# Attention and two MLP layers on one core: the scores of two units issued together from the eighth pair on, and the odd transpose of the tail unit made 128 wide

## The chip, the cores and the metric

One NeuronCore of a Trainium2 chip runs the program. The metric is the device time of one execution in microseconds; the kernel before took 975.68 us (median of three runs, 975.42 to 976.11).

## What is computed

Attention over 4 batches and 8 heads, 576 positions, 64 columns per head, then two MLP layers on 2304 tokens, all in fp32:

```
scores = q k^T / sqrt(D) + min(bias, 0),  bias = -(cum[i] - cum[j]),  cum = cumsum(max(s, 0))
attn   = softmax(scores, causal)
x      = attn v                       # 2304 x 512
x      = leaky_relu(x w_in, 0.01) w_out      # 512 -> 2048 -> 512
out    = softplus(x w2_in) w2_out            # 512 -> 2048 -> 512
```

## The kernel before

The work of the attention stage goes by **pairs** of heads, 16 of them; the two heads of a pair lie in the lower and the upper 64 partitions. A pair has four **units** of queries, in this order: block 3 (queries 384 to 511, four blocks of keys, 512 columns), the tail (the last 64 queries of both heads, 576 keys, laid out as two halves of 288 columns), block 2 (384 columns), and blocks 1 and 0 (256 and 128 columns). Each unit goes through: `scores` on TensorE (lines 311 and 297; Q.K, then a second matmul with BQ and BK that adds the decay; scores use 64 rows of the array, both heads side by side), `maxima` on VectorE (line 332, it also writes the scaled scores into the SBUF tile `sc`), `exps` on ScalarE (line 344), `divisors` on VectorE (lines 350 and 351), `norm` on GpSimd (line 355), `transpose` on TensorE (lines 372, 367 and 363, whole array) into a PSUM tile `pt_t`, and `evacuate`, a copy into PA, PB or PZ: on ScalarE (line 384) for the even half of a unit and for both halves of block 3, on VectorE (line 386) for the rest. `pv` (line 403, 64 columns of the array) multiplies the copies with V. Most of these come in two halves, j = 0 and 1, for the two heads; for the tail unit the even half has four transposes (line 367) and the odd half one (line 363).

The order of all engines is written out by hand in one loop over steps n. In step n the scores of unit n+1 are issued, unit n goes through maxima and exps, unit n-1 is normalised, unit n-2 is transposed, and the last copy of unit n-3 is made. `tick()` runs what earlier steps put off. In the middle of each step `fill.step(n)` issues one half of an MLP matmul group of the first layer (a **chunk**: six matmuls of 512 columns, lines 145 and 614) for a batch that is done; it also loads and splits weights in some steps. A group's two halves fill one PSUM bank (tag `m`, one buffer), which ScalarE empties one tick after the second half. Output groups are not issued before all four hidden tiles are ready; until then a step has no chunk. PV comes at the end of every second step.

Three pools matter: `sc` has three buffers, the transposes' PSUM tag `t` has two, and each of the score tags `s0` and `s1` has two.

After the last pair come the rest of the first layer and the second layer, from about 246 us to the end: MLP matmuls without a break.

Of the kernel before, what the change touches and what calls it, by code (L numbers as in the profile page):

```python
# [18 lines left out]
P = 128  # L19
# [6 lines left out]
def view(t, offset, *dims):  # L26

    return bass.AP(t.tensor, t.offset + offset, [list(t.ap[0])] + [list(d) for d in dims])
# [3 lines left out]
def attn_moe_moe(ctx, tc, q, k, v, s, w1i, w1o, w2i, w2o, out):  # L32
    nc = tc.nc

    B, H, S = s.shape
# [7 lines left out]
    NP = B * NPAIR  # L43
    NB = S // P
    TL = S - NB * P
# [26 lines left out]
    def tick():  # L72
        clock[0] += 1
        for fn, args in todo.pop(clock[0], ()):
            fn(*args)
# [5 lines left out]
    def move(dst, src, queue=nc.sync):  # L81
        queue.dma_start(dst.bitcast(F32), src.bitcast(F32))
# [72 lines left out]
    def attention(att, ps, fills):  # L155
        ident = att.tile([P, P], F32, tag="ident", name="ident")
# [5 lines left out]
        two = lambda nm, shape, dt=F32: [att.tile(shape, dt, tag=f"{nm}{i}", name=f"{nm}{i}") for i in range(2)]  # L162
# [7 lines left out]
        PZ = att.tile([P, 2, TL], F32, tag="PZ", name="PZ")  # L170
# [5 lines left out]
        one = view(V[1], 0, [1, S])  # L176
        s0, s1 = (view(att.tile([P, 2, 512], F32, tag="sc", name="sc", bufs=3), 0, [1, S]) for _ in range(2))
# [52 lines left out]
            nc.sync.dma_start(c_d, c1)  # L230

        def zeros():
            nc.gpsimd.memset(PZ[TL:], 0.0)

        def heads(p):
            b, hp = divmod(p, NPAIR)
# [2 lines left out]
        def load(p, nm, queue=nc.sync, c=slice(None)):  # L239
            if p < NP:  # L240
                t, x = {"q": (Q, q), "k": (K, k), "v": (V, v)}[nm]
                queue.dma_start(t[p % 2][:, c], x[p, :, c])

        def rows(p):

            if p < NP:
                b, hs = heads(p)
                for j in range(2):
                    h, r = b * H + hs.start + j, j * D
                    move(BK[p % 2][r:r + 2], bb_d[h, :, :SB])  # L250
                    move(BQ[p % 2][r + 32:r + 34], bb_d[h, :, :SB])

        def decays(p):

            if p < NP:
                o = c_d.offset + p * 2 * S
                for j in range(2):
                    nc.sync.dma_start(M[p % 2][j * D:(j + 1) * D], bass.AP(c_d.tensor, o + j * S, [[0, D], [1, S]]))
# [8 lines left out]
        def bias(p):  # L267
            if 0 < p < NP:
                m = M[p % 2]
                nc.vector.tensor_scalar(m, m, CQ[:, p:p + 1], None, op0=ALU.subtract)  # L270
                later(1, nc.gpsimd.tensor_tensor, m[:, SB:], m[:, SB:], maskl[:, SH - TL:], ALU.add)


        class Unit:
# [82 lines left out]
            def transpose(self, j):  # L357
                sc = self.sc
                pt = ps.tile([P, 512], F32, tag="t", name="pt_t", bufs=2)
                if self.last:  # L360
                    sc = view(sc, 0, [1, S])
                    if j:
                        nc.tensor.transpose(pt[:TL, :P], sc[:, NB * P:S], ident)
                        self.outs = PZ[:TL], pt[:TL, :P].rearrange("p (j x) -> p j x", x=TL)
                        return
                    for c in range(NB):
                        nc.tensor.transpose(pt[:, c * P:(c + 1) * P], sc[:, c * P:(c + 1) * P], ident)  # L367
                    self.outs = PA[:, :, :, P:], pt.rearrange("p (c j x) -> p j c x", j=2, x=TL)
                    return
                n = self.W // P  # L370
                for c in range(n):
                    nc.tensor.transpose(pt[:, c * P:(c + 1) * P], sc[:, j, c * P:(c + 1) * P], ident)  # L372
                src = pt[:, :self.W].rearrange("p (c x) -> p c x", x=P)
                if n == NB:
                    self.outs = PA[:, j, :, :P], src
                else:
                    k = len(self.subs)
                    self.outs = PB[:, j, :, (2 - k) * P:(3 - k) * P], src
# [9 lines left out]
        def pv(p, last):  # L388

            b, hp = divmod(p, NPAIR)  # L390
            pt = ps.tile([P, 512], F32, tag="a", name="pt_v", bufs=1)
            if last:
                q0, n = (NB - 1) * P, P + TL
                mms = [(c, PA[:, :, c, :], 0, n) for c in range(NB)] + [(NB, PZ, P, TL)]
            else:

                q0, n = 0, (NB - 1) * P
                mms = [(0, PB[:, :, 2, :P], 0, P)] + [
                    (c, PB[:, :, c, max(0, c - 1) * P:], max(c, 1) * P, (3 - max(c, 1)) * P) for c in range(NB - 1)
                ]  # L400
            for m, (c, x, o, w) in enumerate(mms):
                for j in range(2):
                    nc.tensor.matmul(  # L403
                        pt[j * D:(j + 1) * D, o:o + w], V[p % 2][:, c, j, :], x[:, j, :],
                        start=m == 0 or (not last and m == 1), stop=m == len(mms) - 1 or (not last and m == 0),
                    )
            c = slice(b * S + q0, b * S + q0 + n)

            def high():
                nc.scalar.activation(xh[:, hp, c], pt[:, :n], AF.Copy)  # L410
                later(1, low)

            def low():
                nc.vector.tensor_tensor(xl[:, hp, c], pt[:, :n], xh[:, hp, c].bitcast(F32), op=ALU.subtract)
                if not last and hp == NPAIR - 1 and b < B - 1:
                    fill.ready(b)

            later(1, high)
# [22 lines left out]
        fill = fills()  # L441
# [13 lines left out]
        order = [[NB - 1], [], [NB - 2], [1, 0]]  # L455
        units = [(p, ts) for p in range(NP) for ts in order]
        live = {}

        def start(n):
            if n < len(units):  # L460
                live[n] = Unit(*units[n])
                live[n].scores()

        start(0)
        for n in range(len(units) + 3):
            p, i = divmod(n, len(order))
            u0, u1, u2, u3 = (live.get(n - d) for d in range(4))
            if u3:
                u3.evacuate(1)
            start(n + 1)  # L470
            if u0:
                u0.maxima(0)
                u0.exps(0)
            if u1:
                u1.divisors()
                u1.norm(0)
            if u2:
                u2.transpose(0)
            if i == 0:
                bias(p)  # L480
                if p:
                    load(p + 1, "q")
                    load(p + 1, "k")
                    rows(p + 1)
                    decays(p + 1)
            tick()
            if n == len(units):
                fill.free = [("m", 1), ("s0", 2), ("s1", 2)]
            if n:
                fill.step(n)  # L490
            if u0:
                u0.maxima(1)
            if u2 and u0 and u0.last:
                u2.evacuate(0)
            if u0:
                u0.exps(1)
            if not n:
                parts()
                rows(1)
                decays(1)  # L500
                fill.step(n)
            if n == 1:
                columns()
            if u1:
                u1.norm(1)
            if u2:
                if not (u0 and u0.last):
                    u2.evacuate(0)
                u2.transpose(1)
            if i == 3 and p + 1 < NP:  # L510
                load(p + 1, "v")
            elif i in (0, 2) and p:
                pv(p - 1, i == 0)
            if n >= len(units):
                fill.run()
            tick()


    class Fill:
# [117 lines left out]
    fill = fills[0]  # L637
# [67 lines left out]
    behind = []  # L705
# [66 lines left out]
    start = {}  # L772
    for n, st in enumerate(steps):
        start.setdefault(st[:2], n)
    for gi, (layer, g) in enumerate(groups[1:]):
        a, z = start[groups[gi]], start[layer, g]
# [33 lines left out]
def lay_out(name, a):  # L810


    import numpy as np

    if name not in ("q", "k", "v"):
        return np.ascontiguousarray(a)
    B, H, S, D = a.shape
    n, tl = S // P, S % P
    a = a.reshape(B * H // 2, 2, S, D)
    if name == "v":  # L820
        r = np.zeros((B * H // 2, P, n + 1, 2, D), a.dtype)
        r[:, :, :n] = a[:, :, :n * P].reshape(-1, 2, n, P, D).transpose(0, 3, 2, 1, 4)
        r[:, :tl, n] = a[:, :, n * P:].transpose(0, 2, 1, 3)
        return r
    a = a.transpose(0, 1, 3, 2)
    if name == "q":
        more = a[:, ::-1, :, n * P:]
    else:
        more = np.stack([a[:, 1, :, :S // 2], a[:, 0, :, S // 2:]], 1)
    return np.concatenate([a, more], -1).reshape(B * H // 2, 2 * D, -1)  # L830
# [20 lines left out]
```

## Time and profile before

| | |
|---|---|
| median of three runs | 975.68 us |
| the profiled execution | 976.11 us |
| its span in the profile | 974.3 us |
| TensorE matmuls busy | 967.0 us (99%) |
| VectorE, ScalarE, GpSimd busy | 529.3, 536.1, 576.2 us |

All engines' times are those of one execution. The span runs from the first to the last instruction; the profiled execution's own time has 1.8 us around it. TensorE's matmuls overlap each other, so the start of one to the start of the next is what a matmul costs, not its duration.

### The profile page before, as it was taken

What the parts mean: (1) busy time and instruction counts of PE and PEld (TensorE: products, weight loads), DVE (VectorE), ACT (ScalarE), POOL (GpSimd) and SP (SyncE); (2) the same over time, 40 slices, a digit from 0 to 9 for tenths busy, and PEclk for the clock granted to TensorE, in tenths of its full rate; (3) what the DMA queues carried; (4) which work ended last, traced back from release to release, by engine and by line L of the source; (5) the groups of instructions that cost most, each with busy time, mean ns of one, the idle gap of its engine ahead of it and who ended that gap; (6) DMA issues with size and microseconds to landing.
All of it is one profiled execution on the core that took longest, in us unless ns stands there. A gap on an engine that the chain in (4) does not pass through costs nothing.

```text
span 974.3 us, 14738 instructions
## 1 busy us (share of the span) xinstructions
PE 967.0 (99%) x5268; PEld 785.0 (81%) x5268; DVE 529.3 (54%) x1140; ACT 536.1 (55%) x1119; POOL 576.2 (59%) x568
## 2 busy tenths in 40 slices
PE   9999999999999999999999999999999999999998
PEld 6666777777998888888888888888888888888886
DVE  7888566554122222222325358666688868764434
ACT  6888677565453333333344456766656655654452
POOL 7788556443454444344535556777677767774554
PEclk9999999999999999999999999999999999999999
DMA  6444452420621111111102110211011101100202
GB/s 230 156 160 140 134 170 77 143 73 23 218 85 43 44 44 43 35 52 44 44 23 65 44 44 22 65 39 48 22 44 45 64 23 44 44 0 1 87 22 87
DMA packets 37774, 68.06 MB, mean 70 GB/s; under 512 B 3018, under 2 KB 20298, under 8 KB 37700
## 3 DMA queue, kind: packets, MB, share of 16 engines
q1 hardware_dynamic: 37268, 66.36, 21.2%
q8 instruction: 42, 0.69, 0.3%
q10 hardware_dynamic: 432, 0.75, 0.2%
q14 instruction: 32, 0.26, 0.1%
HBM read 59.01 MB, written 8.09 MB: 69 GB/s over the span
## 4 chain that ended last, share of the span: by engine, by line
PE 97%; DVE 1%; POOL 1%; ACT 0%; issue 0%; DMA 0%; DVEq 0%; POOLq 0%
PE ps_h L145 41%; PE ps_out L752 37%; PE pt_s L311 5%; PE pt_v L403 4%; PE pt_t L372 4%; PE ps_o L614 3%; PE pt_t L367 1%; PE pt_s L297 1%; PE pt_w L191 0%; POOL sc L355 0%; DVE sc L332 0%; POOL wil L133 0%; DVE acc L764 0%; DVE PA L386 0%; ACT sc L344 0%
## 5 line engine op out<-in xcount | busy, mean ns | idle before, releaser
L151 POOL TENSOR_TENSOR gl<-gf,gh 128x512 fp32r<-128x512 f32 (+2 forms) x148 | 182.6, 1234 | 150.5 <-ACT gh L150 140.8
L145 PE MATMUL ps_h<-xh,wih 128*128 128x512 f32 (+2 forms) x640 | 237.5, 371 | 0.0
L145 PE MATMUL ps_h<-xh,wil 128*128 128x512 f32 (+2 forms) x640 | 235.8, 368 | 0.0
L145 PE MATMUL ps_h<-xl,wih 128*128 128x512 f32 (+2 forms) x640 | 235.6, 368 | 0.0
L764 DVE TENSOR_TENSOR acc<-ps_out,acc 128x512 f32<-128x512 f32 (+1 forms) x115 | 73.8, 657 | 164.2 <-PE ps_out L752 164.2
L711 POOL TENSOR_TENSOR t<-e,t 128x512 f32<-128x512 f32 (+1 forms) x80 | 112.2, 1403 | 72.2 <-DVE t L710 71.4
L355 POOL TENSOR_SCALAR sc<-sc,st 128x512 f32<-128x512 f32 (+4 forms) x160 | 89.0, 567 | 82.7 <-DVE st L351 76.2
L145 PEld LDWEIGHTS ps_h<-xh,wil 128*128 128x128 f32 x640 | 120.5, 188 | 19.7
L145 PEld LDWEIGHTS ps_h<-xh,wih 128*128 128x128 f32 x640 | 120.6, 188 | 19.3
L145 PEld LDWEIGHTS ps_h<-xl,wih 128*128 128x128 f32 x640 | 120.6, 189 | 19.1
L695 ACT ACTIVATE gf<-ps_h 128x512 f32<-128x512 f32 (+2 forms) x68 | 37.3, 548 | 177.4 <-PE ps_h L145 174.6
L150 ACT ACTIVATE gh<-gf 128x512 fp32r<-128x512 f32 (+2 forms) x148 | 86.1, 582 | 49.1 <-DVE gf L721 48.5
L752 PE MATMUL ps_out<-woh,gl 128*128 128x512 f32 x289 | 112.5, 389 | 0.0
L752 PE MATMUL ps_out<-wol,gh 128*128 128x512 f32 x289 | 112.4, 389 | 0.0
L752 PE MATMUL ps_out<-woh,gh 128*128 128x512 f32 x289 | 112.4, 389 | 0.0
L123 POOL TENSOR_TENSOR wm<-wm,wt 128x512 int32<-128x512 int32 x64 | 85.2, 1332 | 30.7 <-DVE wm L120 30.7
L344 ACT ACTIVATE sc<-sc,st 128x512 f32<-128x512 f32 (+2 forms) x144 | 83.4, 583 | 31.4 <-DVE st L350 20.1
L752 PE MATMUL ps_out<-gh,wol 128*128 128x512 f32 (+2 forms) x272 | 99.1, 364 | 0.0
L752 PE MATMUL ps_out<-gh,woh 128*128 128x512 f32 (+2 forms) x272 | 99.1, 364 | 0.0
L752 PE MATMUL ps_out<-gl,woh 128*128 128x512 f32 (+2 forms) x272 | 99.0, 364 | 0.0
L710 DVE TENSOR_SCALAR t<-e 128x512 f32<-128x512 f32 (+1 forms) x80 | 44.2, 552 | 98.2 <-ACT e L701 98.2
L114 DVE TENSOR_SCALAR wm<-wm 128x512 f32<-128x512 f32 x64 | 38.1, 596 | 92.7 <-ACT wm L108 92.6
(112 smaller groups left out, 1677.1 us busy)
## 6 DMA issues: line engine op xcount, KB each, us to landing
rawi<-in_moe_w_in SPq DMA_DIRECT2D x32, 512.0 KB
rawo<-in_moe_w_out SPq DMA_DIRECT2D x32, 512.0 KB
K<-in_k SPq DMA_DIRECT2D x15, 432.0 KB
V<-in_v SPq DMA_DIRECT2D x16, 320.0 KB
Q<-in_q SPq DMA_DIRECT2D x15, 320.0 KB
out<-acc SPq DMA_DIRECT2D x17, 256.0 KB
M<-c_d SPq DMA_DIRECT2D x30, 144.0 KB
part<-o SPq DMA_DIRECT2D x12, 256.0 KB
```

The lines of the kernel that those rows point to most:

```text
L123: nc.gpsimd.tensor_tensor(m, m, t, op=ALU.add)
L145: nc.tensor.matmul(ps, a, b, start=kk == 0 and n == 0, stop=kk == KD - 1 and n == 2)
L150: nc.scalar.activation(gh, gf, AF.Copy)
L151: nc.gpsimd.tensor_tensor(gl, gf, gh.bitcast(F32), op=ALU.subtract)
L311: nc.tensor.matmul(self.ps[j][:, c], x[r, t * P:(t + 1) * P], y[r, :(t + 1) * P], start=x is Q[i], stop=x is bq,)
L344: nc.scalar.activation(x, x, AF.Exp, scale=-1.0, bias=self.stat(0, e + self.last), accum_out=self.stat(1, e))
L355: nc.gpsimd.tensor_scalar(x, x, self.stat(2, e), 1.0, op0=ALU.mult, op1=ALU.mult)
L372: nc.tensor.transpose(pt[:, c * P:(c + 1) * P], sc[:, j, c * P:(c + 1) * P], ident)
L710: nc.vector.tensor_scalar(t, e, 1.0, -1.0, op0=ALU.add, op1=ALU.add)
L711: nc.gpsimd.tensor_tensor(t, e, t, op=ALU.subtract)
L752: nc.tensor.matmul(u, a, v, start=f == 0 and m == 0, stop=f == G - 1 and m == 2 and j == k - 1)
L764: nc.vector.tensor_tensor(d[..., x], o[..., x], d[..., x], op=ALU.add)
```

## The change

From pair 7 on (`wide = 7`, steps 28 to 63) two steps become one **double step** `two(n)`. In it unit n is called x, n+1 y, n-1 b, n-2 a and n-3 z. A **first double** (n divisible by 4) issues the scores of block 3 and the tail, and transposes block 2 (a) and blocks 1, 0 (b) of the pair before; a **second double** issues block 2 and blocks 1, 0, and transposes block 3 (a) and the tail (b). Each has two chunks. Steps before pair 7 and after the last pair go through `one(n)`, which is the loop's old body.

Besides, the tail unit's odd transpose takes the last 128 columns of its scores instead of the last 64, so that it is 128x128; the copy then reads partitions 64 to 127. PZ is zero in its lower half instead of its upper one, and V's last block is laid out to match.

```diff
         def zeros():
-            nc.gpsimd.memset(PZ[TL:], 0.0)
+            nc.gpsimd.memset(PZ[:P - TL], 0.0)
...
                     if j:
-                        nc.tensor.transpose(pt[:TL, :P], sc[:, NB * P:S], ident)
-                        self.outs = PZ[:TL], pt[:TL, :P].rearrange("p (j x) -> p j x", x=TL)
+                        nc.tensor.transpose(pt[:, :P], sc[:, S - P:S], ident)
+                        self.outs = PZ[P - TL:], pt[P - TL:, :P].rearrange("p (j x) -> p j x", x=TL)
                         return
...
+        wide = 7
...
+        def ahead(p, i):
+            if i == 0:
+                bias(p)
+                if p:
+                    load(p + 1, "q")
+                    load(p + 1, "k")
+                    rows(p + 1)
+                    decays(p + 1)
+
+        def behind(p, i, at):
+            if p and i % 2 == at:
+                pv(p - 1, i == at)
+            if i == 3 and p + 1 < NP:
+                load(p + 1, "v")
...
+        def two(n):
+            p, i = divmod(n, len(order))
+            start(n)
+            start(n + 1)
+            y, x, b, a, z = (live[n - d] for d in range(-1, 4))
+            z.evacuate(1)
+            b.divisors()
+            b.norm(0)
+            x.maxima(0)
+            x.exps(0)
+            a.transpose(0)
+            ahead(p, i)
+            tick()
+            fill.step(n)
+            x.maxima(1)
+            a.evacuate(0)
+            x.exps(1)
+            b.norm(1)
+            a.transpose(1)
+            tick()
+            for j in range(2):
+                y.maxima(j)
+                y.exps(j)
+            x.divisors()
+            x.norm(0)
+            b.transpose(0)
+            a.evacuate(1)
+            tick()
+            fill.step(n + 1)
+            x.norm(1)
+            b.evacuate(0)
+            b.transpose(1)
+            behind(p, i + 1, 1)
+            tick()
+
+        start(0)
+        for n in range(len(units) + 3):
+            if n == len(units):
+                fill.free = [("m", 1), ("s0", 2), ("s1", 2)]
+            if n not in range(len(order) * wide, len(units)):
+                one(n)
+            elif n % 2 == 0:
+                two(n)
...
-        r[:, :tl, n] = a[:, :, n * P:].transpose(0, 2, 1, 3)
+        r[:, P - tl:, n] = a[:, :, n * P:].transpose(0, 2, 1, 3)
```

TensorE, from PV of a pair's last queries to the next chunk, before (pt_v and PA, PZ are PV's, pt_s the scores, pt_t the transposes; ps_o is a chunk):

```order
L403 MATMUL pt_v<-PA,V_97 64x192 x8
L403 MATMUL pt_v<-PZ,V_97 64x64 x2
L311 MATMUL pt_s<-K_88,Q_86 128x384 x2
L311 MATMUL pt_s<-BK_92,BQ_90 128x384 x2
L372 MATMUL pt_t<-ident,sc 128x128 x3
L614 MATMUL ps_o<-gh,woh 128x512
```

and the same place of the change:

```order
L403 MATMUL pt_v<-PA,V_97 64x192 x8
L403 MATMUL pt_v<-PZ,V_97 64x64 x2
L311 MATMUL pt_s<-K_88,Q_86 128x384 x2
L311 MATMUL pt_s<-BK_92,BQ_90 128x384 x2
L311 MATMUL pt_s<-K_88,Q_86 128x256 x2
L311 MATMUL pt_s<-BK_92,BQ_90 128x256 x2
L311 MATMUL pt_s<-K_88,Q_86 128x128 x2
L311 MATMUL pt_s<-BK_92,BQ_90 128x128 x2
L372 MATMUL pt_t<-ident,sc 128x128 x4
```

The scores of blocks 1 and 0 have moved in front of the transposes; they used to come a chunk and six transposes later.

VectorE in a second double of the change, with the semaphores that each instruction waits for (sc_1508 and st_1509 are y's scores and statistics, st_1483 x's statistics, pt_t_1521 the tail's even transposes; 128x1 reads a maximum out):

```order
L332 ISA sc_1508,st_1509<-pt_s_1468,mask_105 128x256 [waits PE_49,Pool_49]
L332 ISA st_1509 128x1
L332 ISA sc_1508,st_1509<-pt_s_1468,mask_105 128x128
L332 ISA st_1509 128x1
L332 ISA sc_1508,st_1509<-pt_s_1469,mask_105 128x256
L332 ISA st_1509 128x1
L332 ISA sc_1508,st_1509<-pt_s_1469,mask_105 128x128
L332 ISA st_1509 128x1
L350 TENSOR_SCALAR st_1483<-st_1483 128x2 [waits Activation_49]
L351 RECIPROCAL st_1483<-st_1483 128x2 [waits DVE_49]
L386 COPY PA_99<-pt_t_1521 128x8x64 [waits PE_49]
```

Before, the maxima of the two halves stood in two halves of a step, and only those of the second half stood in front of this copy (here sc_1525 is the unit's score tile and pt_t_1534 the tail's even transposes):

```order
L332 ISA sc_1525,st_1526<-pt_s_1471,mask_105 128x256
L332 ISA st_1526 128x1
L332 ISA sc_1525,st_1526<-pt_s_1471,mask_105 128x128
L332 ISA st_1526 128x1
L386 COPY PA_99<-pt_t_1534 128x8x64 [waits PE_49]
```

All four maxima and x's divisors are now in front of the copy. The first maximum waits for TensorE (PE_49): for the last transpose of unit a, whose buffer sc_1508 takes.

TensorE at the end of the same double, from the tail's even transposes on:

```order
L367 MATMUL pt_t<-ident,sc 128x128 [waits Pool_49]
L367 MATMUL pt_t<-ident,sc 128x128
L662 MATMUL ps_o<-gh,woh 128x512
L662 MATMUL ps_o<-gl,woh 128x512
L662 MATMUL ps_o<-gh,wol 128x512
L662 MATMUL ps_o<-gh,woh 128x512
L662 MATMUL ps_o<-gl,woh 128x512
L662 MATMUL ps_o<-gh,wol 128x512
L363 MATMUL pt_t<-ident,sc 128x128 [waits DVE_49]
L403 MATMUL pt_v<-PB,V_97 64x128 x2
```

The odd transpose (line 363) now waits for VectorE, for the copy that ends the fence above: it writes into the PSUM buffer that this copy frees. In a first double the odd transposes of blocks 1 and 0 wait in the same way for VectorE's copy of block 2's odd half into PB, which stands behind y's two maxima and x's divisors. PV follows directly behind the odd transposes.

## Rows read from the trace of the kernel before

**Rows 1.** The page, parts 1, 2 and 4: engines, granted clock, chain.

```profile
PE 967.0 (99%) x5268; PEld 785.0 (81%) x5268; DVE 529.3 (54%) x1140; ACT 536.1 (55%) x1119; POOL 576.2 (59%) x568
...
PEclk9999999999999999999999999999999999999999
...
PE 97%; DVE 1%; POOL 1%; ACT 0%; issue 0%; DMA 0%; DVEq 0%; POOLq 0%
```

**Rows 2.** Window of a pair: its length, then PE, PEld, DVE, ACT, POOL busy.

```profile
184.31:200.21 15.90, 15.90 (x120) 11.37 (x118) 8.65 (x35) 9.24 (x26) 5.37 (x12) 1.00 0.35 117
```

**Rows 3.** Waits of TensorE, 110 to 246 us: total us, times, longest.

```profile
PE ps_o L614 <- ACT o L618: 0.4, 1, 0.4
PE pt_t L372 <- DVE PA L386: 0.3, 1, 0.3
```

**Rows 4.** Timeline of TensorE: start us, us, line, out<-in, array used, size, count.

```profile
182.33 0.60 PE L372 MATMUL pt_t<-ident,sc 128*128 128x128 f32 x4
...
184.31 1.13 PE L311 MATMUL pt_s<-K,Q 64*128 64x512 f32 x4
184.87 0.80 PE L311 MATMUL pt_s<-BK,BQ 64*128 64x512 f32 x2
185.60 0.66 PE L367 MATMUL pt_t<-ident,sc 128*128 128x128 f32 x4
...
186.33 0.39 PE L614 MATMUL ps_o<-gl,woh 128*128 128x512 f32 x1
...
187.49 0.27 PE L363 MATMUL pt_t<-ident,sc 128*64 128x128 f32 x1
...
194.90 0.49 PE L372 MATMUL pt_t<-ident,sc 128*128 128x128 f32 x3
195.32 0.70 PE L311 MATMUL pt_s<-K,Q 64*128 64x256 f32 x4
195.67 0.47 PE L311 MATMUL pt_s<-BK,BQ 64*128 64x256 f32 x2
195.97 0.39 PE L311 MATMUL pt_s<-K,Q 64*128 64x128 f32 x4
196.11 0.31 PE L311 MATMUL pt_s<-BK,BQ 64*128 64x128 f32 x2
196.35 0.66 PE L372 MATMUL pt_t<-ident,sc 128*128 128x128 f32 x4
```

**Rows 5.** Timeline of VectorE, same columns; in brackets idle us before, and releaser.

```profile
183.07 0.42 DVE L332 CUSTOM_DVE_ANT_0 sc<-pt_s,mask 128x256 f32<-128x256 f32 x1 [1.79 <-PE pt_t L372]
...
183.42 0.28 DVE L332 CUSTOM_DVE_ANT_0 sc<-pt_s,mask 128x128 f32<-128x128 f32 x1
...
183.64 0.16 DVE L350 TENSOR_SCALAR st<-st 128x2 f32<-128x2 f32 x1
183.83 0.17 DVE L351 RECIPROCAL st<-st 128x2 f32<-128x2 f32 x1
...
186.30 0.69 DVE L386 COPY PA<-pt_t 128x512 f32<-128x512 f32 x1 [0.24 <-PE pt_t L367]
...
190.65 0.56 DVE L386 COPY PB<-pt_t 128x384 f32<-128x384 f32 x1 [0.63 <-PE pt_t L372]
191.12 0.45 DVE L332 CUSTOM_DVE_ANT_0 sc<-pt_s,M 128x288 f32<-128x288 f32 x1
191.49 0.08 DVE L332 DVE_READ_ACCUMULATOR2_ANT st<- 128x1 f32 x1
...
192.86 0.51 DVE L332 CUSTOM_DVE_ANT_0 sc<-pt_s,M,st 128x288 f32<-128x288 f32 x1
```

**Rows 6.** Timeline of VectorE and TensorE at the last pair's end.

```profile
232.30 0.69 DVE L386 COPY PA<-pt_t 128x512 f32<-128x512 f32 x1
...
233.13 0.52 PE L372 MATMUL pt_t<-ident,sc 128*128 128x128 f32 x3 [0.34 <-DVE PA L386]
```

**Rows 7.** Groups of ScalarE by form, 100 to 226 us: busy us, mean ns.

```profile
L618 ACT ACTIVATE o<-ps_o 128x512 f32<-128x512 f32 x8 | 4.7, 586 | 0.8 <-ACT sc L344 0.6
```

More of the change, by code (lines that the diff above doesn't have):

```diff
@@ L457, in attention, with one @@
         live = {}
+        wide = 7
         def start(n):
-            if n < len(units):
+            if n < len(units) and n not in live:
                 live[n] = Unit(*units[n])
                 live[n].scores()
-        start(0)
-        for n in range(len(units) + 3):
+        def ahead(p, i):
[11 more added lines that the diff above has]
+                load(p + 1, "v")
+        def one(n):
             p, i = divmod(n, len(order))
@@ L478, in attention @@
                 u2.transpose(0)
[L479 to L485, printed above, removed]
+            ahead(p, i)
             tick()
-            if n == len(units):
-                fill.free = [("m", 1), ("s0", 2), ("s1", 2)]
             if n:
@@ L509, in attention @@
                 u2.transpose(1)
[L510 to L513, printed above, removed]
+            behind(p, i, 0)
             if n >= len(units):
@@ L516, in attention @@
             tick()
+        def two(n):
[9 more added lines that the diff above has]
+            a.transpose(0)
+            ahead(p, i)
+            tick()
[28 more added lines that the diff above has]
+                two(n)
     class Fill:
```

## The prediction, made before the change was run

> **What bounds the kernel now.** I read the page first, then windows of single pairs, the waits, and last the order of instructions on TensorE and VectorE. TensorE is busy 967.0 of 974.3 us at a granted clock of 1.00 in every slice (the 2.4 GHz level), and 97% of the chain that ended last is its own work [rows 1]. In the attention stage the same holds: the pair that begins at 184.31 us takes 15.90 us, and TensorE is busy for all of it, while VectorE and ScalarE are busy for 8.65 and 9.24 [rows 2]. TensorE waits once each for a copy and a store, 0.3 and 0.4 us, both behind the last pair [rows 3]; from 60 to 226 us the view of waits has no row. So a pair costs what TensorE needs to get through its list. The change can win only by making that list cheaper, and every wait that it puts into the list is lost in full. Behind the attention stage TensorE is just as full, so nothing later makes it up.
>
> **What a change of matmul shape costs now.** The list changes between whole-array work (transposes, MLP chunks), scores on 64 rows, and PV on 64 columns. The rows give the price of each change [rows 4]:
> - Leaving: from the bias scores to what comes next is 0.73 us for 512 columns and 0.24 for 128 when transposes come next, on a straight line 0.40 for 256; with scores next it is 0.30. Leaving costs 0.10.
> - Entering: four transposes last 0.60, three 0.49, so one takes 0.11. Three transposes in front of scores take 0.42: two of 0.11 and a last one of 0.20. Entering costs 0.09.
> - First scores after entering: from Q.K to bias scores is 0.56 at 512 columns and 0.35 at 256, on the line 0.245 at 128; in the middle of a block it is 0.14. That is 0.10.
> - First transpose after scores: from 185.60 to the second matmul of the MLP chunk at 186.33 is 0.73; four transposes at 0.11 and one MLP matmul at 0.23 make 0.67. That is 0.06.
>
> **What the change removes.** Without it a pair leaves whole-array work four times, with it twice.
> - Blocks 1 and 0 now follow block 2 in one shape. Leaving (0.10), first transpose (0.06), entering (0.09) and first scores (0.10) go once: 0.35 us a pair, in nine pairs: 3.15.
> - The tail unit now follows block 3. Leaving (0.10), first transpose (0.06) and entering (0.09) go, but 64x128 to 64x64 is a change that no row shows. The bounds are nothing and the dearest change that is shown, 0.10; I take 0.10, since each change of shape in front of a matmul of this group costs about that. It is 0.15 a pair, and there are eight (the scores of the eighth pair's block 3 are already out when the new order begins): 1.2.
> - Sum of the gain: 4.35 us (bounds 4.3 and 5.2).
> - The wide odd transpose costs nothing. The narrow one starts as soon as any other: the five steps from the second MLP matmul at 186.33 to it at 187.49 are 0.232 each [rows 4], as within a chunk. **Here a page disagrees.** The Trainium skill ("TensorEngine Tiling (Array Packing)", Key Properties) says that changing the tiling mode drains the engine. By it the narrow transpose would pay an entering, and 16 wide ones would bring 16 x 0.09 = 1.4 us more. The rows show no such gap, so the sum has none.
> - Zeros in the other half of PZ and V's tail cost the same instructions. The loads of Q, K and the decays stay at the same place; V's load still follows the same PV. No queue is moved past work that it waits for.
>
> **What the change adds: two waits per pair.** VectorE now takes the maxima of the second unit (y) only after the first (x), and y's score tile is the third of three: it takes the buffer of unit a, so its maxima wait for a's last transpose. The trace shows that hold already, 1.79 us long, ended by a transpose: that ended at 182.33 + 0.60 = 182.93, the maximum began at 183.07, so 0.14 later [rows 4, 5]. It costs nothing now, because a whole step lies between it and the next thing that TensorE needs. In the new order VectorE does y's maxima, x's divisors and then the copy on which the last transposes of the same double step wait (the third fence of the section on the change). TensorE meanwhile has only the next unit's even transposes and one MLP chunk.
>
> Second double (issues block 2 and blocks 1, 0; transposes block 3 and the tail), from the end of block 3's odd transposes:
> - VectorE [rows 5]: 0.14 hold; four maxima, two pairs of 183.07 to 183.64 = 1.14; divisors 183.64 to 184.00, less the 0.07 by which a VectorE instruction lets the next begin (183.42 against 183.49) = 0.29; copy 0.69; and 0.14 until TensorE moves, as in [rows 6], where a copy from 232.30 to 232.99 releases a transpose at 233.13. Sum 2.40.
> - TensorE [rows 4]: four transposes and a chunk take 185.60 to 187.49 = 1.89, less 0.06; four transposes before, 0.44; less the 0.60 to the end of those. Sum 1.67.
> - Wait: 0.73 us.
>
> First double (issues block 3 and the tail; transposes block 2 and blocks 1, 0):
> - VectorE [rows 5]: 0.14; first maximum 191.12 to the end of its read-out at 191.57 = 0.45, since the second takes it as a scalar; second 0.51 less 0.07 = 0.44; divisors 0.29; copy 0.56; 0.14. Sum 2.02.
> - TensorE: 1.89 less 0.06 and less one transpose, 1.72; three transposes before, 0.33; less 0.49. Sum 1.56.
> - Wait: 0.46 us.
>
> That is 1.19 a pair and 10.7 us in nine pairs, against 4.35 gained. Behind the waiting transposes stand PV and the next pair's scores, and the next double starts the same chain, so the wait returns each time.
>
> **Smaller terms.** (1) Steps 44 and 61 have no MLP chunk, because the four hidden tiles are not yet ready then. In step 61 the chunk is the cover of a first double's wait, so six matmuls at 0.232 = 1.4 us more are waited; in step 44 it is the chunk ahead of the hold, where VectorE is busy with x's maxima meanwhile, and I take half, 0.7. (2) MLP chunks share one PSUM bank, and between step 45 and 59 the chunk that ends a bank comes first in a double and the next follows after only seven or eight transposes, some 0.8 us. ScalarE's copy out of that bank lasts 0.59 [rows 7], and now stands behind x's exponentials. Where it is late it delays the same chunk by up to 0.4 in the three first doubles 48, 52, 56 and is hidden by the wait above in the second doubles. (3) Weight splits in steps 36 and 46 put two more ScalarE instructions ahead of the copies, up to 0.4 each. (2) and (3) lie between 0 and 2.0; I take 1.0.
>
> **The sum.** -4.35 + 10.7 + 1.4 + 0.7 + 1.0 = +9.45 us. The profiled execution took 976.11 us, so 985.6; the median of the runs shown, 975.68, is 0.43 lower, so 985.1. The bounds: gain 5.2, waits a fifth smaller (8.6) and smaller terms 1.0 give +4.4, so 980; gain 4.3, waits a tenth larger (11.8) and smaller terms 4.1 give +11.6, so 987.
>
> **The rivals.**
> 1. *Faster.* The waits are not there, and only the cheaper list is seen: 975.7 - 4.35 = 971.3. It decides where VectorE's chains are no longer than 1.56 and 1.67 us, or both together at most 0.48 a pair over them. For it: VectorE is busy for little more than half of a pair [rows 2]. Against it: the chain begins at the hold and is one engine's row of instructions, each with its duration. Chance 0.12.
> 2. *Close to even.* Only the second double's wait is real (the first is the one with half the maxima): -4.35 + 9 x 0.73 = +2.2, so 977.9. Chance 0.12.
> 3. *Slower still.* ScalarE becomes the bound: its exponentials and copies for two units stand in one row, and each of 18 doubles waits another 0.5 us at the even transposes for a copy: +9, so 994. Against it: 9.24 busy of 15.90 [rows 2]. Chance 0.06.
> 4. *The narrow transpose does drain.* A change of shape would then be paid where the rows show none, and the wide one brings 16 x 0.09 = 1.4 on top of my sum: 983.7. Chance 0.04. It is the rule of the tiling page named above; the rows at 186.33 to 187.49 speak against it.
>
> **How the numbers follow.** My forecast has a chance of 0.66. A measurement of this kernel can tell about 0.2%, 2 us, from no change: faster means under 973.7, slower over 977.6. Faster is rival 1, 0.12. Rival 2 lies with two fifths of its chance below 977.6, and my forecast with hardly any: same 0.06. The rest, slower, 0.82. The range 977 to 989 leaves out rival 1 (0.12), a part of rival 2 (0.03) and most of rival 3 (0.05).
>
> **What would show it.** In the profile of the changed kernel the pairs from the eighth on should take about 16.6 us instead of 15.90, with TensorE's busy time down by 0.5 a pair. The view of TensorE's waits should name VectorE's copies of PA and PB (line 386) as what the odd transposes (lines 363 and 372) waited for, some nine times 0.7 and nine times 0.5 us. The maxima on 128x256 and 128x288 should start 0.14 behind a transpose's end. I am wrong if those transposes start without a gap behind the MLP chunk, if the gap is ended by ScalarE or GpSimd, or if the scores of blocks 1 and 0 still show 0.35 us from Q.K to bias scores when they follow block 2.

## The result, and the profile after

| | before | after |
|---|---|---|
| median, runs side by side | 975.55 us (975.13 to 976.11) | 989.74 us (988.84 to 990.43) |
| ratio | | 1.0143, 95% interval 1.013 to 1.0155 |
| span of the profiled execution | 974.3 us | 987.8 us |
| forecast | | 985.1 us (977 to 989), slower 0.82 |

The change makes the kernel slower, as forecast, but by 14.2 us where the sum said 9.45, and the result lies just above the range.

The page of the changed kernel, parts 1 and 4, answers to [rows 1]:

```profile
PE 967.7 (98%) x5268; PEld 786.7 (80%) x5268; DVE 533.7 (54%) x1140; ACT 536.4 (54%) x1119; POOL 574.3 (58%) x568
...
PE 91%; DVE 4%; ACT 2%; issue 1%; POOL 1%; DMA 0%; DVEq 0%; POOLq 0%; ACTq 0%
```

The instructions are the same in number. The chain that ended last, 97% TensorE before, now runs for 4% through VectorE and 2% through ScalarE: TensorE waits for them.

Windows of two pairs of the changed kernel, from the scores of one block 3 to the next (columns as in [rows 2]):

```profile
112.46:129.35 16.89, 15.77 (x119) 11.41 (x117) 10.17 (x41) 10.25 (x29) 8.46 (x15) 1.00 0.46 147
196.83:213.71 16.88, 15.96 (x119) 11.55 (x117) 8.67 (x35) 9.91 (x27) 5.40 (x12) 1.00 0.31 101
```

A pair takes 16.9 us instead of 15.90, and TensorE is no longer busy for all of it. Of the 13.5 us between the spans, 13.1 arise between the eighth pair's first scores (91.35 us before, 91.84 after) and the last PV (245.13 and 258.69). The other 0.5 lies ahead of it: every kernel run here began the eighth pair about 0.3 us or more later than before (the section on the prediction says why). From the start of the last PV to the end of the last matmul both need the same 725.4 us.

The view of TensorE's waits in the changed kernel, 0 to 262 us (total us, times, longest); the three kinds that arise only ahead of the eighth pair are left out:

```profile
PE pt_t L372 <- ACT PB L384: 3.8, 3, 2.0
PE pt_t L363 <- DVE PA L386: 3.3, 8, 0.5
PE pt_t L372 <- DVE PB L386: 2.9, 3, 1.8
PE ps_o L662 <- ACT o L666: 1.4, 2, 1.1
...
PE ps_h L145 <- ACT o L666: 0.6, 1, 0.6
PE ps_h L145 <- ACT gf L635: 0.5, 1, 0.5
```

The second and third rows are the forecast's VectorE copies. The others end at ScalarE, and the longest single wait, 2.0 us, is among those.

This view counts idle time only. Below a wait is what lies from one matmul's start to the next, less what that step costs without one: 0.11 us between transposes, 0.23 behind a chunk's matmul [rows 4], 0.03 from transposes to a chunk. A second double step of the changed kernel on VectorE, then on TensorE:

```profile
125.53 0.42 DVE L332 CUSTOM_DVE_ANT_0 sc<-pt_s,mask 128x256 f32<-128x256 f32 x1 [1.94 <-PE pt_t L372]
...
126.64 0.16 DVE L350 TENSOR_SCALAR st<-st 128x2 f32<-128x2 f32 x1
126.84 0.17 DVE L351 RECIPROCAL st<-st 128x2 f32<-128x2 f32 x1
126.92 0.67 DVE L386 COPY PA<-pt_t 128x512 f32<-128x512 f32 x1
```

```profile
124.78 0.60 PE L372 MATMUL pt_t<-ident,sc 128*128 128x128 f32 x4
125.22 0.60 PE L367 MATMUL pt_t<-ident,sc 128*128 128x128 f32 x4
...
126.80 0.40 PE L662 MATMUL ps_o<-gh,wol 128*128 128x512 f32 x1
127.65 0.33 PE L363 MATMUL pt_t<-ident,sc 128*128 128x128 f32 x1 [0.45 <-DVE PA L386]
```

That is the predicted chain: block 3's odd transposes end at 125.38, y's first maximum begins 0.15 later, VectorE's copy ends at 127.59 (both halves of the tail unit are copied by VectorE, the even one into PA), and the tail's odd transpose, which without a wait would begin 0.23 behind 126.80, begins 0.62 late. The release took 0.06 us, not the 0.14 that the sum took from [rows 6].

The first double step of the new order, which the forecast had no term for (VectorE and GpSimd, then ScalarE and TensorE):

```profile
95.23 1.27 DVE L350 TENSOR_SCALAR st<-st 128x4 f32<-128x4 f32 x1 [0.38 <-ACT sc L344]
...
96.75 0.69 DVE L332 CUSTOM_DVE_ANT_0 sc<-pt_s,mask 128x512 f32<-128x512 f32 x1
```

```profile
95.18 1.29 POOL L645 TENSOR_TENSOR gl<-gf,gh 128x512 fp32r<-128x512 f32 x1
```

```profile
97.54 0.72 ACT L344 ACTIVATE sc<-sc,st 128x512 f32<-128x512 f32 x1 [1.82 <-DVE st L332]
...
98.26 0.47 ACT L384 ACTIVATE PB<-pt_t 128x384 f32<-128x384 f32 x1
```

```profile
98.87 0.52 PE L372 MATMUL pt_t<-ident,sc 128*128 128x128 f32 x3 [1.97 <-ACT PB L384]
```

VectorE stands at b's divisors until ScalarE has the old order's last exponentials, then that instruction takes 1.27 us while GpSimd's subtraction runs (the same shape takes 0.17 at 128.34 in this trace). Behind it come x's maxima, behind these x's exponentials on ScalarE, behind these the copy for which TensorE waits 2.1 us. Then TensorE's granted clock falls to its lower level, 1.2 GHz, for a while (0.50 of the full clock from 99.50 to 102.20). The windows show it (PEclk is the number behind GpSimd's):

```profile
98.70:103.00 4.30, 4.13 (x18) 3.11 (x20) 2.10 (x9) 2.57 (x7) 3.02 (x6) 0.60 0.20 68
103.00:112.00 9.00, 8.55 (x73) 6.74 (x71) 3.60 (x19) 5.13 (x17) 2.13 (x4) 1.00 0.08 29
```

At 0.60 of the full clock 4.3 us do the work of 2.6: 1.7 us more. The passage costs 3.8 us.

### The profile page after: what moved, and what is told of

Read it like the earlier page. It is cut to its first block, busy times and chain, and to the rows that moved or that the text cites. A ratio compares the mean times of both kernels' runs of the same rounds, so it can differ in the third digit from the quotient of the medians.

```text
span 987.8 us, 14755 instructions
## 1 busy us (share of the span) xinstructions
PE 967.7 (98%) x5268; PEld 786.7 (80%) x5268; DVE 533.7 (54%) x1140; ACT 536.4 (54%) x1119; POOL 574.3 (58%) x568
## 4 chain that ended last, share of the span: by engine, by line
PE 91%; DVE 4%; ACT 2%; issue 1%; POOL 1%; DMA 0%; DVEq 0%; POOLq 0%; ACTq 0%
PE ps_h L145 39%; PE ps_out L800 36%; PE pt_s L311 5%; PE pt_v L403 4%; PE pt_t L372 3%; PE ps_o L662 3%; DVE sc L332 2%; ACT sc L344 1%; DVE PA L386 1%; PE pt_s L297 1%; POOL sc L355 0%; DMA K<-in_k 0%; PE pt_t L367 0%; PE pt_t L363 0%; DVE st L350 0%
```

## Experiments

**The wide transpose alone.** `wide = NP` keeps the old order for all pairs.

```diff
-        wide = 7
+        wide = NP
```

> The double steps are taken out (all steps run the old body); the 128-wide odd transpose, PZ and V's layout stay. My theory (the wide transpose costs nothing and gains nothing): 975.5, within 0.5 of the kernel before. Rival, the narrow transpose drains the array: 16 x 0.09 us less, 974.1. Second rival, the layout costs something at the start, where the changed kernel's profile stood 0.49 us behind after 91 us: 976.0.

Measured: 976.43 us, ratio 1.0007 (0.9998 to 1.0016), nearest to the second rival's 976.0, though the interval does not tell it from no change. On TensorE the two transposes cost the same: in the pair at 184 us the narrow one begins 0.235 us behind the matmul ahead of it and the next matmul 0.202 behind it; the wide one has 0.232 and 0.201. Rival 4, a drain at the narrow one, falls. The wide one's price lies elsewhere, ahead of the eighth pair, and is read below.

**From the ninth pair on.** Is the passage into the new order what the sum lacked?

```diff
-        wide = 7
+        wide = 8
```

> The double steps begin one pair later. Theory A (the first double step of the new order met a clash: VectorE's divisor row took 1.27 us beside a GpSimd subtraction of 1.29 us, TensorE waited 2.0 us and then ran 3.4 us at half clock): one pair less of the net steady loss (0.7) and most of about 3.6 us of that passage gone, 986; TensorE's clock stays at 1.00. Theory B (any passage from the old to the new order costs this): only 0.7 less, 989.0, with the clock at half again.

Measured: 986.2 us, ratio 1.011 (1.0093 to 1.0127). The view of TensorE's waits names none between 70 and 115 us, where the ninth pair's passage lies too, and the granted clock is 1.00 there. One pair less saves 3.5 us, where a steady pair loses 1.0 (16.9 against 15.9). So the loss belongs to the eighth pair's passage and not to entering the new order as such.

**Copies first.** In `two`, the copies of the second and third transposes go ahead of y's maxima.

```diff
-            for j in range(2):
-                y.maxima(j)
-                y.exps(j)
-            x.divisors()
-            x.norm(0)
             b.transpose(0)
             a.evacuate(1)
+            b.evacuate(0)
+            for j in range(2):
+                y.maxima(j)
+                y.exps(j)
+            x.divisors()
+            x.norm(0)
             tick()
             fill.step(n + 1)
             x.norm(1)
-            b.evacuate(0)
```

> In a double step the copies on which the last transposes wait stand in front of y's maxima on VectorE, and unit b's even transposes are issued before them; nothing else changes. My theory (those transposes wait because VectorE does y's maxima first, held by the third score buffer): the 18 waits at the odd transposes that VectorE ends, 4.8 us in second and 3.2 us in first doubles counted from start to start, go, 981.7. Rival (ScalarE is the bound): the waits come back behind ScalarE's exponentials, 986 or more.

**Four score buffers.** The old order of copies, but y's scores no longer take a's buffer (room comes from one buffer less of the MLP's hidden tiles).

```diff
-name="sc", bufs=3)
+name="sc", bufs=4)
-                self.gpool, self.tpool = new("gpoolA", G + 1), new("tpoolA", 2)
+                self.gpool, self.tpool = new("gpoolA", G), new("tpoolA", 2)
```

> The score tiles get four buffers instead of three (to make room the hidden tiles of the first layer's batches get four buffers instead of five); the order stays. If the hold of y's maxima by the third buffer is what makes the chain too long: VectorE does them ahead of the transposes and the same 8.0 us go, 981.7, without a releasing VectorE copy in TensorE's waits. If the number of VectorE instructions in front of the copy is what counts and not the hold: 988 to 990.

Measured: 983.07 us, ratio 1.0075 (1.006 to 1.009), for the copies first; 982.88, ratio 1.0072 (1.0057 to 1.0087), for four buffers. Both take out the waits of the second double steps, in two different ways, as the theory says: y's maxima, held by the third buffer, stood ahead of the copies on VectorE. TensorE's waits with four buffers:

```profile
PE pt_t L372 <- ACT PB L384: 3.7, 3, 1.9
PE pt_t L372 <- DVE PB L386: 2.0, 3, 1.1
PE ps_o L662 <- ACT o L666: 1.4, 2, 1.1
...
PE pt_t L372 <- DVE PA L386: 0.2, 1, 0.2
```

No row names L363 any more. Both kernels came out some 1.3 us above what was expected. Of the 8 us of waits that should go, counted from start to start, four buffers leave 2.5 at VectorE's copy of PB; the copies first leave 0.6, but the waits at steps 44 and 48 grow from 1.4 and 1.3 to 1.9 each. The passage stays in both (a wait of 2.1 us at 98.7 to 99.0), and so do the waits behind ScalarE, larger than the prediction's second and third small terms. In the profiled execution with the copies first, the granted clock also fell twice, at 98.98 and 163.83 us.

**The passage, taken apart.** First, b's divisors and normalisation behind x's first maxima and exponentials, in that one double step.

```diff
-            b.divisors()
-            b.norm(0)
+            if n > len(order) * wide:
+                b.divisors()
+                b.norm(0)
             x.maxima(0)
             x.exps(0)
+            if n == len(order) * wide:
+                b.divisors()
+                b.norm(0)
```

> In the first double step alone (the eighth pair's), b's divisors and normalisation stand behind x's first maxima and exponentials. Theory A (this passage costs 3.5 us: VectorE stands at the divisors, for ScalarE's last exponentials of the old order and then 1.27 us beside GpSimd, while x's first maxima are ready behind them; ScalarE's copy waits for the maxima, TensorE for the copy, and then the granted clock halves): the maxima move 1.6 us forward, the wait at the even transposes at 98.9 us falls from 2.1 to about 0.5, the clock stays at 1.00, and the time is 986.6 us (985.8 to 987.3). Rival B (the passage is late whatever VectorE's order, because ScalarE or GpSimd is behind there): the wait stays near 2 us and the time at 989.0 to 990.2. Rival C (the wait goes, but the maxima are themselves slowed beside GpSimd's instruction): wait 1.5 us, 988 to 989.

Measured: 988.66 us, ratio 1.0136 (1.0122 to 1.015), 1.1 better than the change by medians and between A and B. The time is the one that rival C named, but not for its reason: the first maximum takes 0.69 us, as in the changed kernel. It begins at 94.83 instead of 96.75, the copy is in time and the clock of the profiled execution stays at 1.00, as A said. But TensorE's timeline now has two waits:

```profile
97.46 0.68 PE L372 MATMUL pt_t<-ident,sc 128*128 128x128 f32 x3 [0.60 <-POOL sc L355]
...
100.92 0.30 PE L372 MATMUL pt_t<-ident,sc 128*128 128x128 f32 x1 [1.36 <-DVE PB L386]
```

and VectorE and GpSimd show why the second is there:

```profile
99.33 0.52 DVE L332 CUSTOM_DVE_ANT_0 sc<-pt_s,M,st 128x288 f32<-128x288 f32 x1 [1.27 <-POOL M L75]
...
100.23 0.54 DVE L386 COPY PB<-pt_t 128x384 f32<-128x384 f32 x1
```

```profile
97.73 1.28 POOL L133 TENSOR_TENSOR wol<-wm,woh 128x512 fp32r<-128x512 f32 x1
98.97 0.32 POOL L75 TENSOR_TENSOR M<-M,maskl 128x64 f32<-128x64 f32 x1
```

The tail's maximum waits for its mask, which GpSimd makes behind the last piece of a weight split. So the same kernel with those splits one step earlier:

```diff
-(21, 23), (23, 25)
+(20, 22), (22, 24)
```

> As the changed kernel with the divisors later in the eighth pair's first double step, and the weight splits of steps 23 and 25 (with their loads) one step earlier, so that GpSimd's last piece of it (1.28 us at 97.73) is out of that double step. Theory (what is left of that passage's loss is GpSimd's queue: y's second maxima waited for the mask that GpSimd makes behind this piece): the wait of 1.36 us at 100.9 shrinks to about 0.4 and the time is 987.7 (987.2 to 988.2), a loss over the other kernel's seven later pairs of what is left there. Rival (the mask waits for VectorE's own part of it and not for the piece, or the earlier split makes TensorE wait in the old order's steps): 988.7 or more.

Measured: 990.78 us, ratio 1.0154 (1.014 to 1.0168). In the passage the two waits, 0.77 and 1.56 from start to start, fall to 0.27 and 0.30: GpSimd's queue is the rest of the cause. But the split now crowds the old order's steps, with waits at 78.09, 87.02 and 88.29 us that the kernels before had not (0.2, 1.4 and 1.0 from start to start), so the theory was right on the wait and the rival on the time, and the whole is slower. The eighth pair is a bad place to begin because GpSimd still carries the weights there, and moving these only moves the wait.

**Is the list cheaper when nothing waits?** From the ninth pair on, with four score buffers, I took all named waits away together. In the first two kernels ScalarE copies the first transposes before x's first exponentials and the second tick comes before the second ones; the copy of the second transposes goes ahead of y's maxima, or between these and x's divisors.

```diff
-            x.exps(0)
             a.transpose(0)
+            a.evacuate(0)
+            x.exps(0)
             ahead(p, i)
             tick()
             fill.step(n)
             x.maxima(1)
-            a.evacuate(0)
+            tick()
             x.exps(1)
             b.norm(1)
             a.transpose(1)
-            tick()
+            a.evacuate(1)
             for j in range(2):
...
             b.transpose(0)
-            a.evacuate(1)
```

> Everything that the runs so far named is taken away together, from the ninth pair on: four score buffers; ScalarE copies the first transposes before x's first exponentials and empties the chunk's bank before the second ones; the copy of the second transposes stands ahead of y's maxima. The theory (the list of TensorE is 0.35 + 0.15 us a pair cheaper, and only these waits ate it): eight pairs give 4.0 us, 975.7 - 4.0 = 971.7, with 1 to 3 us of waits left at steps 46 and 61 (a split, no chunk): 973 to 975, faster than before. Rival (another row of the same engines becomes late in their place, the normalisation on GpSimd for instance, or the gain isn't there when the waits are gone): 976 to 981, and the view of TensorE's waits names the engine.

> As the kernel with the copies first, but the copy of the second transposes stands behind y's maxima and ahead of x's divisors. By the theory 972.5 to 975: VectorE isn't held by those transposes before y's maxima, and the waits that the run with four score buffers left at the copies of PB (0.84 and 1.17 us) shrink by the two divisor instructions, 0.3 us each, and no more. If it is slower than its sister by 1 us or more, VectorE's order behind the transposes still decides; if equal, it doesn't.

Measured: 980.64 us, ratio 1.005 (1.0036 to 1.0063), with the copy first; 984.95, 1.0092 (1.0079 to 1.0106), with it between. The rival held: a new engine came up in both, and the first lies in the rival's range, the second above it. TensorE's waits with the copy first:

```profile
PE pt_t L367 <- POOL sc L355: 3.2, 2, 1.6
PE pt_t L372 <- POOL sc L355: 2.5, 5, 1.0
```

GpSimd's timeline names the reason:

```profile
136.66 1.27 POOL L645 TENSOR_TENSOR gl<-gf,gh 128x512 fp32r<-128x512 f32 x1 [1.43 <-ACT gh L640]
137.91 1.06 POOL L355 TENSOR_SCALAR sc<-sc,st 128x288 f32<-128x288 f32 x2
```

My earlier tick had put the chunk's subtraction, which waits for ScalarE, ahead of the tail's normalisation. Between the sisters VectorE's order still decides 4.3 us. The next kernels issue both normalisations of b together, ahead of the ticks, and the second of them also puts x's exponentials first again.

```diff
             b.divisors()
             b.norm(0)
+            b.norm(1)
...
             x.exps(1)
-            b.norm(1)
```

> The kernel with the copies first, with one move: b's second normalisation is issued with its first, ahead of what the ticks give GpSimd. Theory (the new waits of that kernel, 3.2 us at the tail's even transposes and 2.5 us at others for GpSimd's normalisation, come from GpSimd's subtraction standing ahead of it and waiting for ScalarE's rounding): these 5.7 us go, 980.6 - 5.7 = 974.9, about 2.8 us of waits left at the chunk's bank (0.87 at step 46, 0.54, 0.27 each) and at step 61. Rival (GpSimd itself is full there, 1.27 us for each piece of a split, and the wait only moves to the next transposes): 978 to 980.

> As the kernel with the early normalisation, and x's first exponentials are again ahead of the copy of the first transposes, but both stand ahead of the tick. Theory (ScalarE idles 1.97 us for the first transposes in each double step while x's maxima are long done, so its row ends that much later, and the chunk's bank is emptied late): the bank's waits shrink, 1 to 1.5 us less than its sister: 973.5 to 974. Rival (the copy is late behind the exponentials where a double step has a split or no chunk): 975 to 976, with waits for ScalarE's copy of PB at the transposes of steps 36 and 44.

Measured: 975.07 us, ratio 0.9995 (0.9986 to 1.0004), and 974.99, 0.9993 (0.9984 to 1.0002). Neither can be told from the kernel before. The first is where the theory put it, to 0.2 us: the new waits for GpSimd went, and the view keeps 0.9 at the chunk's bank, 0.4 for VectorE's copy at step 61 and 0.3 for ScalarE's copy at step 44. The second gained nothing to speak of: the bank's wait at step 46 shrank from 0.88 to 0.28, but grew from 0.54 to 0.70 at step 48, and step 44 waits 0.9 from start to start for ScalarE's copy where it waited 0.5, as the rival said of it and of step 36, where none is left.

The last pair of kernels lets step 45 issue two chunks, so that a bank begins and ends within one double step, and differs in the first pair of the new order.

```diff
             self.run()
+            if n == 45:
+                self.run()
...
-            x.exps(0)
+            if n != 44:
+                x.exps(0)
             a.transpose(0)
             a.evacuate(0)
+            if n == 44:
+                x.exps(0)
```

> As the kernel with the exponentials first, with two edits: step 45 issues two chunks, so that from step 46 on both chunks of a bank lie in one double step and PV and scores stand between a bank's end and the next bank's start; and in step 44 ScalarE's copy goes ahead of x's exponentials. Theory (the chunk that ends a bank came first in a double step and the next one 7 or 8 transposes behind it, less than the 0.6 us of ScalarE's copy): the waits for the bank, 0.28 and 0.70 at steps 46 and 48, 0.27 in two later first double steps and 0.06 in six second ones, go, 1.9 us, and 0.3 of 0.8 at step 44; step 60 has no chunk instead of 61 and gives back 0.3 at most: 973.1 us (972.5 to 973.9), clearly faster than before. Rival (the list was never that much cheaper, and a wait comes back somewhere for each that goes): 975.

> The same kernel from the eighth pair on, as the change has it, not the ninth. One pair more gives 0.5 us of list; theory (in the eighth pair's passage GpSimd is full with the last piece of a weight split and the subtraction of a chunk, 1.28 us each, whatever the order of the other engines): TensorE waits 1.5 to 2.5 us there, so 1.0 to 2.0 us slower than its sister: 974.1 to 975.1. Rival (the passage was lost by the changed kernel's order of copies and exponentials, which is mended here): 972.6, half a microsecond faster than its sister.

Measured: **973.21 us**, ratio 0.9976 (0.9967 to 0.9985), from the ninth pair on: the one kernel here that clearly beats before. From the eighth on it is 974.96, ratio 0.9994 (0.9985 to 1.0003), 1.75 us slower than its sister, as the theory said; TensorE's timeline has one wait in that passage:

```profile
98.80 0.52 PE L372 MATMUL pt_t<-ident,sc 128*128 128x128 f32 x3 [1.91 <-POOL sc L355]
```

Windows of the 973.21 us kernel, two pairs:

```profile
186.25:201.63 15.38, 15.38 (x119) 11.52 (x118) 9.35 (x35) 9.81 (x27) 6.76 (x13) 1.00 0.34 111
201.63:217.01 15.38, 15.38 (x119) 11.52 (x117) 9.30 (x35) 10.22 (x28) 7.98 (x14) 1.00 0.30 93
```

A pair takes 15.38 us and TensorE is busy for all of it, as in [rows 2], where it took 15.90. The changed list is 0.52 us cheaper; in the run of the wide transpose alone a pair takes 15.87, so 0.03 of it comes without the merging, and 0.49 stand against 0.35 + 0.15 in the prediction.

## Why the prediction was right in sign and short in size

The waits of the changed kernel, summed from its timeline, beside the terms of the prediction (us):

| term | forecast | measured |
|---|---|---|
| cheaper list | -4.35 | -4.5 (15.90 - 15.38 = 0.52 a pair, split here as 0.35 x 9 + 0.17 x 8) |
| second double steps, copy of PA | 9 x 0.73 = 6.6 | 4.8 (0.20 to 0.62 each) |
| first double steps, copy of PB, with step 61's missing chunk | 9 x 0.46 + 1.4 = 5.5 | 3.3, in three of them: 0.83 (step 32), 0.52 (40), 1.99 (60) |
| ScalarE: steps 36 and 44, the chunk's bank | 0.7 + 1.0 = 1.7 | 5.7: 0.72 (step 36), 1.44 (44), bank 0.60, 1.31, 0.80, 0.79 (46, 48, 52, 56) |
| passage at step 28 | none of its own | 2.1 of wait and 1.7 of clock |
| sum, from the eighth pair to the last PV | +9.45 | +13.1 |

- **The bound and the sign held.** TensorE was full, and each wait that came into its list was lost. The cheaper list is real, but it shows only once the waits are gone. Rival 1 (faster) named the right gain and the wrong premise; rival 2 (close to even) is out by the time, although VectorE's copy made only three of nine first double steps wait. A pair took 16.9 us where 16.6 was forecast. Of the signs of being wrong one showed: in six of the nine first double steps the odd transposes start behind the chunk without a gap. The scores of blocks 1 and 0 do follow in 0.14 us, at 122.53 and 122.67.
- **The step that failed is the sum's tacit one, that all nine pairs are alike.** "That is 1.19 a pair and 10.7 us in nine pairs" treats the first double step, at the change from the old order, like the others. Its inputs were visible before: GpSimd's split pieces of steps 25 to 28, exponentials of the old order that end late, and slow divisors. The sum took 0.16 us for line 350 from one row; in the trace of before 12 of its 64 instructions took 0.31 to 0.95 beside an instruction of GpSimd. The longest:

```profile
145.20 0.95 DVE L350 TENSOR_SCALAR st<-st 128x2 f32<-128x2 f32 x1
```

```profile
144.86 1.27 POOL L597 TENSOR_TENSOR gl<-gf,gh 128x512 fp32r<-128x512 f32 x1
```

The timeline prices the passage at 3.8 us of the 4.7 missed. Starting one pair later saved 3.5 in all, with what the eighth pair gains in its list and waits in its second double step, and the two kernels that take the passage apart show what it is made of.
- **The other 0.9** is the 0.5 ahead of the eighth pair and the differences of single executions from their medians. The 0.5 is a term that the sum put at nothing: the tail's copy with the wide transpose. The prediction counted the same instructions, but the copy that reads partitions 64 to 127 no longer overlaps its neighbours on VectorE, in any pair; why is not shown. Before, then the changed kernel:

```profile
50.55 0.69 DVE L386 COPY PA<-pt_t 128x512 f32<-128x512 f32 x1 [0.23 <-PE pt_t L367]
51.16 0.27 DVE L386 COPY PZ<-pt_t 64x128 f32<-64x128 f32 x1
51.36 0.67 DVE L332 CUSTOM_DVE_ANT_0 sc<-pt_s,mask 128x512 f32<-128x512 f32 x1
```

```profile
50.77 0.69 DVE L386 COPY PA<-pt_t 128x512 f32<-128x512 f32 x1 [0.23 <-PE pt_t L367]
51.49 0.29 DVE L386 COPY PZ<-pt_t 64x128 f32<-64x128 f32 x1
51.81 0.69 DVE L332 CUSTOM_DVE_ANT_0 sc<-pt_s,mask 128x512 f32<-128x512 f32 x1
```

From the copy into PA to the next maximum it is 0.81 us before and 1.04 here, and the run of the wide transpose alone shows the same. Behind that maximum come b's divisors, then GpSimd's normalisation, and for this TensorE waits 0.25 and 0.27 us longer in two early pairs, at 44 and 55 us. The second, before and here:

```profile
55.47 0.68 PE L372 MATMUL pt_t<-ident,sc 128*128 128x128 f32 x3 [0.17 <-POOL sc L355]
```

```profile
55.96 0.68 PE L372 MATMUL pt_t<-ident,sc 128*128 128x128 f32 x3 [0.44 <-POOL sc L355]
```

- **The steady waits were right in sum, 13.8 against 13.8, and not in their parts.** A second double step waits 0.6 rather than 0.73, since the release costs 0.06. In steps 48, 52 and 56 no wait at VectorE's copy is left, because the bank's wait comes first and VectorE catches up meanwhile; that term was mis-sized, 0.4 at most in the text against 0.79 to 1.31, and it is the second step that failed. ScalarE and TensorE in step 48 of the changed kernel:

```profile
183.19 0.72 ACT L344 ACTIVATE sc<-sc,st 128x512 f32<-128x512 f32 x1 [0.25 <-DVE st L332]
...
183.91 0.61 ACT L127 ACTIVATE woh<-wm 128x512 fp32r<-128x512 f32 x1
184.43 0.57 ACT L666 ACTIVATE o<-ps_o 128x512 f32<-128x512 f32 x1
```

```profile
183.17 0.82 PE L372 MATMUL pt_t<-ident,sc 128*128 128x128 f32 x6
185.06 0.50 PE L662 MATMUL ps_o<-gh,woh 128*128 128x512 f32 x1 [1.07 <-ACT o L666]
```

The bank's last chunk is done when the transposes begin at 183.17. Its copy (L666) comes 1.26 us later, behind x's exponentials and a weight split's rounding. The agreement of the sums is luck in part.
- **ScalarE (rival 3)** does not bound the kernel: even transposes wait for its copy in three double steps, not in 18. But the order of its row cost 4.0 us more than the sum gave it (5.7 against 1.7), and the runs that reorder it and keep a bank within a double step gain most of that back: in the 973.21 us kernel 1.4 of the 5.7 is left.
- **Rival 4** is out, by the rows and the run of the wide transpose alone.

On the slow divisors, what the trace shows first: VectorE's 128x4 instruction on L350 ends at 96.50, GpSimd's subtraction at 96.47, and in the kernel with the divisors later L350 begins at 95.45, takes 0.98 and ends 0.03 behind GpSimd again. The Trainium skill ("SBUF — State Buffer", Who interferes with whom) says that VectorE in some modes and GpSimd share one port pair, held for a whole instruction, and that the later one blocks; these rows agree.

## What to carry to other kernels

Where an engine is full, a cheaper list is worth exactly what its waits leave: before merging steps, write down for each waiting instruction the row of its releaser's engine, and mend buffers and order on VectorE, ScalarE and GpSimd together, since each mended row here (VectorE's copies, then GpSimd's normalisation, then the bank on ScalarE) brought up the next. Price the step in which a new order begins by itself, with the work that the old one still has in its queues. A loop that alternates halves of a shared buffer should have both halves between the same long stretches of other work.

## What was not expected of the hardware

- An instruction on 128x4 elements took 1.27 us on VectorE beside a 1.29 us instruction on GpSimd, and 1.31 beside the same one in the kernel with four buffers; alone the same line takes 0.17 on 128x4.
- After the wait of 1.97 us idle at 98.87, TensorE's granted clock fell to the lower level; so it did in the kernel with the copies first, twice. There the idle waits were 2.00 and 1.69. After idle waits of 1.95 at 98.66 in the kernel with four buffers, of 1.91 in the last one and of 1.82 at 236.95 in the changed kernel itself it stayed at the upper level. In the last kernel three of eleven executions, at 975.9 to 976.1 us, have a mean granted clock of 0.998, as the profiled execution of the changed kernel has, and the other eight, at 974.1 to 975.5, one of 0.999 or 1.000. That would fit a fall in some executions of one program and not in others, but no trace of those three shows it. What tells these apart is open; no run was made for it.
